# Polysketch attention and an ELU layer on one core: the first two query groups by squares of sums and differences

## The chip, the cores and the metric

One core of a Trainium2 chip. The metric is device time in microseconds (us) of one execution; lower is better. Work is shared by five engines with queues of their own: TensorE (PE, matrix products; PEld are its weight loads), VectorE (DVE), ScalarE (ACT), GpSimd (POOL) and SyncE (SP), which issues most transfers. SBUF is the working memory of 128 partitions; matmuls write to PSUM, which has eight banks of 128 x 512 fp32.

## The reference

Inputs: q, k, v of shape (4, 4, 1088, 32) in fp32, two sketches S1 and S2 of 8 x 32, and the two weights of the dense layer, 128 x 2048 and 2048 x 128. The sketches and the dense weights arrive as 64-bit floats (the divisions by a NumPy square root make them so).

```python
def phi(x):
    a = np.einsum('rd,bhsd->bhsr', S1, x)
    b = np.einsum('rd,bhsd->bhsr', S2, x)
    return np.einsum('bhsi,bhsj->bhsij', a, b).reshape(*x.shape[:-1], r * r)
q_p, k_p = (phi(q), phi(k))
kv = np.einsum('bhsf,bhsd->bhfd', k_p, v)
z = np.sum(k_p, axis=2)
num = np.einsum('bhsf,bhfd->bhsd', q_p, kv)
den = np.einsum('bhsf,bhf->bhs', q_p, z)[..., None] + 1e-06
attn = num / den
x = attn.transpose(0, 2, 1, 3).reshape(B * S, H * D)        # 4352 x 128
h = x @ w_in
g = np.where(h > 0.0, h, np.exp(np.minimum(h, 0.0)) - 1.0)
return g @ w_out
```

So each token has 64 features per head, the products of 8 sketch values a_i with 8 sketch values b_j.

## The kernel before

**Tiling.** The 4352 tokens are 68 half tiles of 64, taken in groups of eight (512 tokens): g = 0 to 7 are two groups for each batch element, and a last group holds the four half tiles left over. The 2048 hidden units are eight steps cp of 256, so a step (g, cp) is `mm1` (L840: two 128-unit halves into two PSUM banks, each in four 32-column tiles by `quarters`, L253), `elu_a` (L854: relu and exp on ScalarE), `elu_d` (L865: one VectorE instruction that writes gg) and `mm2` (L876) or a scheme with seven products (L770). The weights come as 64-bit words and are rounded on the chip: RA (VectorE, L102), RB (ScalarE, L107), RS, RM, RD, RE (VectorE, L117, L121, L129, L137). Number i of RA(i) and the others counts pieces: 0 and 1 are the first weight (w_in) of steps 0 and 1, 2 and 3 their second (w_out), 4 and 5 the two of step 2, and from 6 on whole steps.

**Order.** The order on each engine is written out by hand (`manual_schedule`): the order of the calls in the program is the order of every engine's queue. From L946 to L1000 stands the prologue: keys of batch element 0 are turned (`transp`, L279) and sketched (`KF`, L336), their products are formed (`KO_pool` on GpSimd, `KO_first` on VectorE, L416), z is summed (`Z_first`, `Z`, `Z_out`, which writes the third part of SW, L465), and kv is summed in the bank tagged o1 (`KA`, L428).

**Groups 0 and 1.** `q1_first` and `q1z_first` (L505, L517) or `q1_second` (L526) sketch the queries with tokens on the 128 partitions. `q2_den` (L581) makes the denominator, its reciprocal and an, the sketch a divided by it. `q2_out` (L599) forms the 64 products per token and head on VectorE (qp). `q4_early` (L612) turns qp by eight transposes on TensorE, copied out by ScalarE (L622). `q5_early` (L624) multiplies by kv (`KS_first`, L479, turns kv), and ScalarE copies the result to xg (L634), the input of `mm1`. `keep_warm` (L260) issues filler matmuls. Then `mm1_first` (L847) is step (0, 0), followed in the prologue by (0, 1) and the first `mm2`.

**After the prologue** the loop at L1108 runs the remaining steps from (1, 0) on, with `mm2` two steps behind `mm1`; `KT_out` (L441) of batch element 0 turns kv out of PSUM on VectorE and writes it to DRAM for later groups. Groups from 2 on get their queries in another way (`queries`, L706), between steps.

PSUM banks are handed out by tag: h (four), aux (two), o0 and o1 (one each); a new tile of a tag waits for the readers of the one it replaces.

Of the kernel before, what the change touches and what calls it, by code (L numbers as in the profile page):

```python
# [27 lines left out]
def kernel(  # L28
# [21 lines left out]
    nc = tc.nc  # L50
# [282 lines left out]
    kv_ps, feats, wzs, kf_ps = {}, {}, {}, []  # L333


    def KF(b):  # L336
# [91 lines left out]
    def KA(b, halves=(0, 1)):  # L428
# [4 lines left out]
        for i in range(0 if 0 in halves else 5, KT if 1 in halves else 5):  # L433
# [51 lines left out]
    NH = B * NT
    NQ = (NH + 7) // 8
# [9 lines left out]
    def half_tile(g, k):  # L496
        return (g // 2, 8 * (g % 2) + k) if g < NQ - 1 else (k, NT - 1)


    def q1_first():  # L500
        p = psum.tile([P, 512], F32, name="abqp", tag="aux")
        for i in range(4):
            for u in range(2):
                b, t = half_tile(0, 2 * i + u)
                nc.tensor.matmul(p[64 * u:64 * u + 64, i * 64:i * 64 + 64], qT[b][:, t, :],  # L505
                                 Sab[:].rearrange("p h y -> p (h y)"),
                                 skip_group_check=True, tile_position=(0, 64 * u))
        abw[0] = work.tile([P, H * 4, 2 * R], F32, name="abq", tag="abq", bufs=1)
        nc.scalar.copy(abw[0][:].rearrange("p (h t) y -> p h t y", h=H),
                       p[:, :256].rearrange("p (t h y) -> p h t y", t=4, h=H))  # L510

    def q1z_first():
        p = psum.tile([P, 512], F32, name="zqp", tag="h", bufs=4)
        for i in range(4):
            for u in range(2):
                b, t = half_tile(0, 2 * i + u)
                nc.tensor.matmul(p[64 * u:64 * u + 64, i * 32:i * 32 + 32].rearrange("p (h r) -> p h r", h=H),  # L517
                                 qT[b][:, t, :], SW[:, :, 2, :], skip_group_check=True, tile_position=(0, 64 * u))
        return p[:, :128].rearrange("p (t h r) -> p h t r", t=4, h=H)

    def q1_second():
        p = psum.tile([P, 512], F32, name="abwp", tag="h", bufs=4)
        for i in range(4):
            for u in range(2):
                b, t = half_tile(1, 2 * i + u)
                nc.tensor.matmul(p[64 * u:64 * u + 64, i * 96:i * 96 + 96], qT[b][:, t, :],  # L526
                                 SW[:].rearrange("p h x r -> p (h x r)"), skip_group_check=True,
                                 tile_position=(0, 64 * u))
        abw[1] = work.tile([P, H * 4, 3 * R], F32, name="abw1", tag="abq1", bufs=1)
        nc.scalar.copy(abw[1][:].rearrange("p (h t) y -> p h t y", h=H),  # L530
                       p[:, :384].rearrange("p (t h y) -> p h t y", t=4, h=H))
# [67 lines left out]
    def q2_out(g, parts=1, between=None):  # L599
        m = H * qn[g]  # L600
        x, an = abw.pop(g), ans.pop(g)
        qp[g] = work.tile([P, 4 * H, R, R], F32, name="qp", tag="qp", bufs=2)
        for i in range(parts):
            if i and between:
                between()
            h = slice(i * m // parts, (i + 1) * m // parts)
            a_ = an[:, h]
            b_ = x[:, h, :R]
            nc.vector.tensor_mul(qp[g][:, h], _ap(a_, list(a_.ap[1:]) + [[0, R]]),  # L609
                                 _ap(b_, [b_.ap[1], [0, R], b_.ap[2]]))  # L610

    def q4_early(g):  # L612

        qpT[g] = work.tile([P, H, 2, P], F32, name="qpT", tag="qpT", bufs=2)
        for hh in range(2):
            p = psum.tile([P, 512], F32, name="qtp", tag="aux")
            for h2 in range(2):
                for m in range(2):
                    o = (h2 * 2 + m) * P
                    r = (2 * hh + h2) * 4 + 2 * m  # L620
                    nc.tensor.transpose(p[:, o:o + P], qp[g][:, r:r + 2].rearrange("p t i j -> p (t i j)"), ident[:])  # L621
            nc.scalar.copy(qpT[g][:, 2 * hh:2 * hh + 2], p[:].rearrange("p (h m s) -> p h m s", h=2, m=2))  # L622

    def q5_early(g):  # L624
        xp = [psum.tile([P, 512], F32, name="xps", tag="aux") for _ in range(2)]
        for h in range(H):
            for w in range(2):
                nc.tensor.matmul(xp[w][D * h:D * h + D, :256], kvS[64 * w:64 * w + 64, h, :],  # L628
                                 qpT[g][64 * w:64 * w + 64, h].rearrange("p m s -> p (m s)"),
                                 skip_group_check=True, tile_position=(64 * w, D * h))  # L630
        xg[g] = work.tile([P, 512], F32, name="xg", tag="xg", bufs=3)
        to = xg[g][:].rearrange("p (m w s) -> p w m s", w=2, s=P)
        for w in range(2):
            nc.scalar.copy(to[:, w], xp[w][:, :256].rearrange("p (m s) -> p m s", s=P))  # L634
# [211 lines left out]

    def mm1_first():  # L847
        hs[0, 0] = [psum.tile([P, 512], F32, name="h", tag="h", bufs=4) for c in range(2)]
        for w in range(2):
            for c in range(2):  # L850
                cols = [x[:].rearrange("p (m w s) -> p w m s", w=2, s=P)[:, w] for x in (hs[0, 0][c], xg[0])]
                quarters(cols[0], W[:, 0, c * P:c * P + P], cols[1])
# [351 lines left out]
```

## Time and profile before

| | |
|---|---|
| median of 3 runs | 261.91 us (261.74 to 262.23) |
| the profiled execution | 262.34 us |
| its span, first to last instruction | 260.6 us |
| granted TensorE clock | 0.998 |
| first `mm1` starts | 16.25 us |
| first `mm2` ends | 23.51 us |
| busy: PE, DVE, ACT, POOL | 254.8, 186.9, 183.4, 159.0 us |

How to read it: an instruction row has its start and duration in us, the engine, the line of the kernel, the operation, output<-input by the program's names, and the shape. "x16" counts instructions; an fp32 matmul call is two of them, a transpose one. "[0.45 <-ACT e L863]" is idle time ahead of the instruction and what ended it. A chain of waits is followed back from the last instruction: each step names what the next one waited for. A busy PE need not be one at its peak, as matmuls are pipelined and their ends are modelled.

### The profile page before, as it was taken

The page shows a single profiled execution, that of the slowest core. Times are in us where ns is not written, and L with a number is a line of the kernel's source. Part 1 is how long each engine was busy: PE and PEld are TensorE (multiplying, and loading weights), DVE is VectorE, ACT ScalarE, POOL GpSimd, SP SyncE. Part 2 cuts the span into 40 slices and gives each one's busy share as a digit, 9 for nine tenths or more (in the row PEclk, how much of TensorE's full clock was granted, in tenths as well). Part 3 has the DMA queues.
Part 4 walks back from the last instruction along what each step waited for, and adds up shares of the span by engine and source line. Part 5 has one row for each costly group of instructions (what it writes and reads, how often), then busy time and mean ns, then how long its engine had stood idle before and what let it go on. Part 6 is the DMA issues. An engine that isn't in the chain of part 4 may idle for free.

```text
span 260.6 us, 9756 instructions
## 1 busy us (share of the span) xinstructions
PE 254.8 (98%) x4123; PEld 158.4 (61%) x4123; DVE 186.9 (72%) x352; ACT 183.4 (70%) x358; POOL 159.0 (61%) x202
## 2 busy tenths in 40 slices
PE   8899999999999999999999999999999999999994
PEld 6753333453346667666666666665666666668993
DVE  6799999999988967997477675744466746544651
ACT  2379968766667577776687777775877777777792
POOL 3520007002179996788678798888688888887310
PEclk9999999999999999999999999999999999999999
DMA  5998079012112210002100204220001110110021
GB/s 173 330 358 222 3 223 268 24 21 85 28 18 28 31 34 18 3 15 34 20 0 4 33 10 104 60 30 13 3 3 27 34 26 3 25 19 3 3 30 33
DMA packets 30379, 15.61 MB, mean 60 GB/s; under 512 B 22496, under 2 KB 28000, under 8 KB 30336
## 3 DMA queue, kind: packets, MB, share of 16 engines
q1 hardware_dynamic: 29904, 14.63, 23.0%
q8 instruction: 32, 0.52, 0.9%
q10 hardware_dynamic: 368, 0.30, 0.3%
q0 software_dynamic: 64, 0.07, 0.1%
q14 instruction: 11, 0.09, 0.1%
HBM read 11.31 MB, written 2.36 MB: 52 GB/s over the span
## 4 chain that ended last, share of the span: by engine, by line
PE 97%; DVE 1%; ACT 0%; issue 0%; DVEq 0%
PE h L256 45%; PE pb L790 17%; PE pa L790 13%; PE o L256 5%; PE pb L766 4%; PE ol L256 3%; PE idle L264 1%; PE kv L435 1%; PE abp L343 1%; PE h L681 1%; PE h L551 1%; PE qtp L621 1%; DVE qp L609 1%; PE h L693 1%; PE xps L628 0%; PE kfps L365 0%
## 5 line engine op out<-in xcount | busy, mean ns | idle before, releaser
L256 PE MATMUL h<-xg,W 128*32 128x512 f32 (+3 forms) x904 | 130.8, 539 | 0.4 <-ACT xg L634 0.4
L869 DVE SCALAR_TENSOR_TENSOR gg<-e,h 128x512 f32<-128x512 f32 x128 | 85.9, 681 | 52.6 <-ACT e L863 47.8
L861 ACT ACTIVATE e<-h 128x512 f32<-128x512 f32 x128 | 75.5, 590 | 46.2 <-PE h L256 46.0
L863 ACT ACTIVATE e<-e 128x512 f32<-128x512 f32 x128 | 80.9, 632 | 3.8
L751 POOL TENSOR_TENSOR tt<-gg 128x512 f32<-128x512 f32 x50 | 64.3, 1286 | 28.9 <-DVE gg L869 25.2
L256 PEld LDWEIGHTS h<-xg,W 128*32 128x32 f32 (+1 forms) x904 | 43.0, 122 | 43.0 <-issue 34.4
L754 POOL TENSOR_TENSOR tt<-gg,tt 128x256 f32<-128x256 f32 x50 | 36.9, 739 | 3.9
L753 POOL TENSOR_TENSOR tt<-tt,gg 128x256 f32<-128x256 f32 x50 | 36.7, 734 | 3.9
L790 PEld LDWEIGHTS pa<-gg,W 128*64 128x64 f32 (+1 forms) x496 | 23.7, 126 | 22.4 <-issue 22.2
L790 PE MATMUL pa<-gg,W 128*64 128x128 f32 (+1 forms) x496 | 30.6, 274 | 0.0
L790 PE MATMUL pb<-tt,SS 128*64 128x128 f32 (+1 forms) x480 | 29.6, 273 | 0.0
L790 PEld LDWEIGHTS pb<-tt,SS 128*64 128x64 f32 (+1 forms) x480 | 22.8, 126 | 0.0
L790 PE MATMUL pa<-tt,SS 128*32 128x128 f32 (+1 forms) x288 | 21.2, 273 | 0.0
L790 PE MATMUL pb<-gg,SS 128*64 128x128 f32 (+1 forms) x256 | 19.9, 273 | 0.0
L790 PE MATMUL pb<-tt,W 128*64 128x128 f32 (+1 forms) x256 | 19.9, 273 | 0.0
L134 POOL TENSOR_TENSOR raw<-raw,tiny 128x512 f32<-128x512 f32 x1 | 1.0, 1041 | 24.7 <-DVE raw L129 24.7
L256 PE MATMUL o<-gg,W 128*32 128x512 f32 x128 | 15.3, 595 | 0.0
L790 PEld LDWEIGHTS pa<-tt,SS 128*32 128x32 f32 (+1 forms) x288 | 13.7, 124 | 0.0
L790 PEld LDWEIGHTS pb<-gg,SS 128*64 128x64 f32 (+1 forms) x256 | 12.8, 125 | 0.0
L790 PEld LDWEIGHTS pb<-tt,W 128*64 128x64 f32 (+1 forms) x256 | 12.8, 125 | 0.0
L766 PE MATMUL pb<-gg,W 128*32 128x256 f32 x192 | 11.5, 380 | 0.0
L921 DVE SCALAR_TENSOR_TENSOR gg<-e,h 128x256 f32<-128x256 f32 x16 | 6.6, 418 | 6.4 <-PE h L256 3.2
(163 smaller groups left out, 269.3 us busy)
## 6 DMA issues: line engine op xcount, KB each, us to landing
raw<-in_moe_w_in_dram SPq DMA_DIRECT2D x8, 256.0 KB, 6.3
raw<-in_moe_w_out_dram SPq DMA_DIRECT2D x8, 256.0 KB, 6.5
out_dram<-ob SPq DMA_DIRECT2D x112, 16.0 KB, 1.5
hd_k<-in_k_dram SPq DMA_DIRECT2D x3, 544.0 KB, 7.5
hd_q<-in_q_dram SPq DMA_DIRECT2D x3, 544.0 KB, 8.5
v<-in_v_dram SPq DMA_DIRECT2D x4, 288.0 KB, 7.1
v<-in_v_dram SPq DMA_DIRECT2D x4, 256.0 KB, 8.4
raw<-qpF SPq DMA_DIRECT2D x16, 64.0 KB, 2.0
```

Source lines behind the costliest of these rows:

```text
L256: nc.tensor.matmul(dst[c:c + tile], lhs[:, c:c + tile], rhs, skip_group_check=True, tile_position=(0, c), **kw)
L264: nc.tensor.matmul(idle[c:c + tile, :cols], ones[:, :tile], ones[:, :cols], skip_group_check=True, tile_position=(0, c))
L343: nc.tensor.matmul(ps[i // 5][64 * u:64 * u + 64, 64 * (i % 5):64 * (i % 5) + 64], kT[b][:, u * KT + i, :], Sab[:].rearrange("p h y -> p ( ...
L751: nc.gpsimd.tensor_tensor(_ap(t[:, 0], [[4 * P, 2], [P, 2], [1, P]]), _ap(gs[g, cp][:, 0, P:], [[4 * P, 2]] + us), _ap(gs[g, cp][:, 0], [[ ...
L753: nc.gpsimd.tensor_tensor(t[:, 1], t[:, 2], b11, op=ADD)
L754: nc.gpsimd.tensor_tensor(t[:, 3], b21, t[:, 1], op=SUB)
L766: nc.tensor.matmul(acc[1][0][r:r + width[0], 256 * hi:256 * hi + 256], lhs[:, w:w + width[0]], gg[:, c, 256 * u:256 * u + 256], start=(cp ...
L790: nc.tensor.matmul(bank[r:r + width[0], P * col:P * col + P], lhs[:, w:w + width[0]], rhs[:, u], start=(first and i in ((0,) if g == 1 els ...
L861: nc.scalar.activation(e, hs[g, cp][c][:, :n], RELU, scale=-1.0)
L863: nc.scalar.activation(e, e, EXP, scale=-1.0)
L869: nc.vector.scalar_tensor_tensor(gs[g, cp][:, c, :n], es[g, cp][:, c, :n], -1.0, hs[g, cp][c][:, :n], op0=ADD, op1=MAX)
L921: nc.vector.scalar_tensor_tensor(gs["last", k // 2][:, k % 2, :2 * P], es["last", k // 2][:, k % 2, :2 * P], -1.0, hs["last", k][:, :2 * P ...
```

## The change

It uses 4ab = (a+b)^2 - (a-b)^2. For groups 0 and 1 the feature products are no longer formed on VectorE. `make_Spm` builds, on VectorE, weights whose 128 columns are the 64 sums S2_i + S1_j and the 64 differences, on all four heads' 32 rows. `q_sums` multiplies them with the queries as they lie (32 dimensions of a head on 32 partitions): four matmuls of 32 rows by 128 columns, a head each, side by side in the array. `q_squares` squares each result from PSUM to SBUF on ScalarE. kv stands twice on the 128 partitions, scaled by +1/4 and -1/4 (`KS_copy`), so `x_sums` needs one matmul of 128 rows per head. The denominator still comes from sketches with tokens on the partitions (`az`, `den_a`, `den_b`); `den_out` brings its reciprocal to the layout of x by 16 small matmuls with the identity, `den_copy` takes it to SBUF, and `x_out` on VectorE multiplies it in while it writes xg. The transposes, the fillers from `Z_out` on, and the copies to xg go. `KA` is cut in two, the squares and weight roundings are woven in between in a new order, `KT_out(0)` reads the SBUF copy of kv, and the second half of the q transpose comes earlier.

```diff
+    quarters_pm = const.tile([P, 1], F32, name="qpm")
+    nc.gpsimd.memset(quarters_pm[:64], 0.25)
+    nc.gpsimd.memset(quarters_pm[64:], -0.25)
...
+    def make_Spm():
+        for s, op in enumerate((ADD, SUB)):
+            nc.vector.tensor_tensor(Spm[:, s], _ap(sps[:, R:], [[1, R], [0, R]]), _ap(Sc[:], [[0, R], [1, R]]), op=op)
...
-        nc.vector.transpose(kt[:], kv_ps[b][:, :R * R])
+        nc.vector.transpose(kt[:], kv_ps[b][:, :R * R] if b else kds[0][:, 0])
...
+    def KS_copy():
+        nc.scalar.mul(kvS[:].rearrange("p h d -> p (h d)"), kv_ps[0][:, 128:256], quarters_pm[:])
...
+    def q_sums(g, half=None):
+        c = slice(0, 512) if half is None else slice(256 * half, 256 * half + 256)
+        for h in range(H):
+            if not half:
+                tag = "o0" if h == 3 else "h" if g or h == 2 else "aux"
+                sums[g, h] = psum.tile([P, 512], F32, name="qs", tag=tag, bufs={"o0": 1, "h": 4, "aux": 2}[tag])
+            rows = slice(32 * h, 32 * h + 32)
+            nc.tensor.matmul(sums[g, h][:, c], Spm[rows].rearrange("p s i j -> p (s i j)"),
+                             tokens(g, rows, c.start // 64, c.stop // 64), skip_group_check=True, tile_position=(32 * h, 0))
+
+    def q_squares(g, h):
+        if h % 2 == 0:
+            sq[g, h // 2] = work.tile([P, 2, 512], F32, name="sq", tag=("qp", "qpT")[g], bufs=2)
+        nc.scalar.square(sq[g, h // 2][:, h % 2], sums.pop((g, h))[:])
...
+    def az_copy(g):
+        abw[g] = work.tile([P, H, 4, R], F32, name="aq", tag=f"aq{g}", bufs=1)
+        nc.scalar.copy(abw[g][:], dens[g][:, :, :, 0, :])
...
+    def den_out(g, **kw):
+        ps = rbs[g] = psum.tile([P, 512], F32, name="rb", **kw)
+        for t in range(4):
+            for h in range(H):
+                nc.tensor.matmul(ps[32 * h:32 * h + 32, P * t:P * t + P], _ap(dens[g][:, 4 * h + t:], [[0, D]]), ident[:],
+                                 skip_group_check=True, tile_position=(0, 32 * h))
...
+    def x_sums(g, parts, half, **kw):
+        if half == 0:
+            xp[g] = psum.tile([P, 512], F32, name="xps", **kw)
+        c = slice(512 // parts * half, 512 // parts * (half + 1))
+        for h in range(H):
+            nc.tensor.matmul(xp[g][D * h:D * h + D, c], kvS[:, h, :], sq[g, h // 2][:, h % 2, c],
+                             skip_group_check=True, tile_position=(0, D * h))
+
+    def x_out(g, parts, half):
...
+        nc.vector.tensor_mul(xg[g][:, c], xp[g][:, c], rb_all[0][:, g, c])
...
     transp(qT, "q", 0, 0, 8)
-    zps, zl = Z_first()
-    q1_first()
+    make_Spm()
+    q_sums(0, 0)
+    zps = Z_first()
+    zl = ZC(0, zps)
     KO_pool()
     KO_first(4, 5)
     KO_first(5, 7)
+    q_sums(0, 1)
     Z(0, zps, zl)
+    q_squares(0, 0)
+    KA_first((4, 5, 6), True)
     Z_out(0, zps)
     KO_first(7, KT)
-    keep_warm(1, 96, 64)
-    zq = q1z_first()
-    q2_den(0, zq, lambda: RA(0))
-    q2_out(0, 2, lambda: RA(1))
-    KA(0)
-    KS_first()
-    keep_warm(1)
+    q_squares(0, 1)
+    az(0, zps)
+    KA_first((0, 1, 2, 3, 7, 8), False)
+    RA(0)
+    az_copy(0)
+    q_squares(0, 2)
+    transp(qT, "q", 0, 8, NT)
     RB(0)
+    den_a(0)
+    den_b(0)
+    az(1)
+    KS_kd()
+    q_squares(0, 3)
+    KS_turn()
+    den_out(0, tag="aux", bufs=2)
+    az_copy(1)
+    RA(1)
+    RS(0)
+    den_a(1)
+    den_b(1)
+    for f in (RM, RD, RE):
+        f(0)
+    KS_copy()
+    den_copy(0)
+    q_sums(1)
+    x_sums(0, 2, 0, tag="aux", bufs=2)
+    x_sums(0, 2, 1)
+    den_out(1, tag="o1", bufs=1)
     RB(1)
-    q4_early(0)
-    transp(qT, "q", 0, 8, NT)
-    RC_2()
-    RE(0)
-    RE(1)
-    q1_second()
-    q5_early(0)
-    keep_warm(1, 192, width[0])
+    for h in range(H):
+        q_squares(1, h)
+    x_out(0, 2, 0)
+    x_out(0, 2, 1)
     mm1_first()
-    q2(1, 2, lambda: RA(2))
+    RA(2)
     RB(2)
-    elu_a(0, 0, 0)
-    elu_a(0, 0, 1, (0,))
-    mm1(0, 1, (0,))
-    q4_early(1)
+    for f in (RS, RM, RD, RE):
+        f(1)
+    RA(3)
+    for f in (RS, RM, RD, RE):
+        f(2)
+    elu_a(0, 0, 0, (0,))
+    den_copy(1)
+    elu_a(0, 0, 0, (1,))
+    elu_a(0, 0, 1)
+    x_sums(1, 1, 0, tag="aux", bufs=2)
+    mm1(0, 1)
     elu_d(0, 0, 0)
-    mm1(0, 1, (1,))
-    elu_a(0, 0, 1, (1,))
-    RC(2)
-    RA(3)
-    elu_a(0, 1, 0, (0,))
+    x_out(1, 1, 0)
     RB(3)
-    q5_early(1)
     elu_d(0, 0, 1)
     mm2(0, 0, True, False)
```

More of the change, by code (lines that the diff above doesn't have):

```diff
@@ L304 @@
     nc.gpsimd.tensor_copy(SW[:, :, :2, :].rearrange("p h x r -> p h (x r)"), Sab[:])
+    Sc = const.tile([FD, R], F32, name="Sc")
+    nc.scalar.copy(Sc[:], sps[:, :R])
+    Spm = const.tile([FD, 2, R, R], F32, name="Spm")
+    def make_Spm():
+        for s, op in enumerate((ADD, SUB)):
+            nc.vector.tensor_tensor(Spm[:, s], _ap(sps[:, R:], [[1, R], [0, R]]), _ap(Sc[:], [[0, R], [1, R]]), op=op)
     Sxp = const.tile([FD, 2, 2, R], F32, name="Sxp")
@@ L332 @@
     kvd = {b: dram.tile([P, 2 * D], F32, name=f"kvd{b}")[:] for b in range(B)}
-    kv_ps, feats, wzs, kf_ps = {}, {}, {}, []
+    kv_ps, feats, wzs, kds, kf_ps = {}, {}, {}, {}, []
     def KF(b):
@@ L439, in KA, with KA_first @@
                 z_tile(b, kv, i)
+    def KA_first(tiles, first):
+        if first:
+            kv_ps[0] = psum.tile([P, 512], F32, name="kv", tag="o1", bufs=1)
+        for i in tiles:
+            for h in range(H):
+                nc.tensor.matmul(kv_ps[0][32 * h:32 * h + 32, :R * R], vt[0][:, (h * KT + i) * D:(h * KT + i + 1) * D],
+                                 feats[0, i // 5][:, i % 5, h].rearrange("p i j -> p (i j)"),
+                                 start=(first and i == tiles[0]), stop=(not first and i == tiles[-1]),
+                                 skip_group_check=True, tile_position=(0, 32 * h))
     def KT_out(b):
         kt = work.tile([P, 2 * D], F32, name="kvt", tag="kvt")
-        nc.vector.transpose(kt[:], kv_ps[b][:, :R * R])
+        nc.vector.transpose(kt[:], kv_ps[b][:, :R * R] if b else kds[0][:, 0])
         nc.sync.dma_start(kvd[b], kt[:])
@@ L476, in Z_first, with KS_kd, KS_turn @@
             z_tile(0, ps, i)
-        return ps, ZC(0, ps)
-    def KS_first():
-        kd = work.tile([P, 2, R * R], F32, name="kd", tag="kd", bufs=1)
+        return ps
+    def KS_kd():
+        kd = kds[0] = work.tile([P, 2, R * R], F32, name="kd", tag="kd", bufs=1)
         nc.scalar.copy(kd[:], _ap(kv_ps[0][:, :R * R], [[0, 2], [1, R * R]]))
-        nc.tensor.transpose(kv_ps[0][:, 128:256], kd[:].rearrange("p w f -> p (w f)"), ident[:])
-        nc.scalar.copy(kvS[:].rearrange("p h d -> p (h d)"), kv_ps[0][:, 128:256])
+    def KS_turn():
+        nc.tensor.transpose(kv_ps[0][:, 128:256], kds[0][:].rearrange("p w f -> p (w f)"), ident[:])
+    def KS_copy():
+        nc.scalar.mul(kvS[:].rearrange("p h d -> p (h d)"), kv_ps[0][:, 128:256], quarters_pm[:])
     NH = B * NT
@@ L497, in half_tile, with tokens @@
         return (g // 2, 8 * (g % 2) + k) if g < NQ - 1 else (k, NT - 1)
-    def q1_first():
-        p = psum.tile([P, 512], F32, name="abqp", tag="aux")
+    sums, sq, dens, rbs, xp = {}, {}, {}, {}, {}
+    rb_all = {}
+    def tokens(g, rows, t0=0, t1=8):
+        b, t = half_tile(g, t0)
+        return qT[b][rows, t:t + t1 - t0, :].rearrange("p t s -> p (t s)")
+    def q_sums(g, half=None):
[7 more added lines that the diff above has]
+                             tokens(g, rows, c.start // 64, c.stop // 64), skip_group_check=True, tile_position=(32 * h, 0))
@@ L502, in q1_first, with az @@
+    def q_squares(g, h):
+        if h % 2 == 0:
+            sq[g, h // 2] = work.tile([P, 2, 512], F32, name="sq", tag=("qp", "qpT")[g], bufs=2)
+        nc.scalar.square(sq[g, h // 2][:, h % 2], sums.pop((g, h))[:])
+    def az(g, p=None):
+        if p is None:
+            p = psum.tile([P, 512], F32, name="azp", tag="h", bufs=4)
         for i in range(4):
             for u in range(2):
-                b, t = half_tile(0, 2 * i + u)
-                nc.tensor.matmul(p[64 * u:64 * u + 64, i * 64:i * 64 + 64], qT[b][:, t, :],
-                                 Sab[:].rearrange("p h y -> p (h y)"),
+                b, t = half_tile(g, 2 * i + u)
+                nc.tensor.matmul(p[64 * u:64 * u + 64, 128 + i * 64:192 + i * 64].rearrange("p (h y) -> p h y", h=H),
+                                 qT[b][:, t, :], SW[:, :, 1:, :].rearrange("p h x r -> p h (x r)"),
@@ L507, in q1_first @@
                                  skip_group_check=True, tile_position=(0, 64 * u))
[L508 to L531, printed above, removed]
+        dens[g] = p[:, 128:384].rearrange("p (t h x r) -> p h t x r", t=4, h=H, x=2)
@@ new lines, in az_copy, with den_a, den_b @@
+    def az_copy(g):
+        abw[g] = work.tile([P, H, 4, R], F32, name="aq", tag=f"aq{g}", bufs=1)
+        nc.scalar.copy(abw[g][:], dens[g][:, :, :, 0, :])
+    def den_a(g):
+        pw = pws[g % 2]
+        nc.vector.tensor_mul(pw[:, :4 * H, :R].rearrange("p (h t) r -> p h t r", h=H), abw.pop(g)[:], dens[g][:, :, :, 1, :])
+    def den_b(g):
+        pw = pws[g % 2]
+        den = dens[g] = work.tile([P, 4 * H], F32, name="dn", tag="den", bufs=2)
+        nc.vector.tensor_reduce(den[:], pw[:, :4 * H], axis=AX, op=ADD)
+        nc.vector.reciprocal(den[:], den[:])
@@ new lines, in den_out, with den_copy @@
+    def den_out(g, **kw):
[3 more added lines that the diff above has]
+                nc.tensor.matmul(ps[32 * h:32 * h + 32, P * t:P * t + P], _ap(dens[g][:, 4 * h + t:], [[0, D]]), ident[:],
+                                 skip_group_check=True, tile_position=(0, 32 * h))
+    def den_copy(g):
+        if not rb_all:
+            rb_all[0] = work.tile([P, 2, 512], F32, name="rbc", tag="kp", bufs=3)
+        nc.scalar.copy(rb_all[0][:, g], rbs.pop(g)[:])
@@ new lines, in x_sums @@
+    def x_sums(g, parts, half, **kw):
[6 more added lines that the diff above has]
+    def x_out(g, parts, half):
+        if half == 0:
+            xg[g] = work.tile([P, 512], F32, name="xg", tag="xg", bufs=3)
+        c = slice(512 // parts * half, 512 // parts * (half + 1))
+        nc.vector.tensor_mul(xg[g][:, c], xp[g][:, c], rb_all[0][:, g, c])
@@ L575, in q1_out @@
                                 ps[r][:, o:o + 32 * m])
-    def q2(g, parts=1, between=None):
-        q2_den(g, None, between)
-        q2_out(g, parts)
     def q2_den(g, zq=None, between=None):
@@ L597, in q2_den @@
         ans[g] = an
[L599 to L634, printed above, removed]
     exch = [raw_2[:, c].bitcast(F32).rearrange("p (e m a) w -> p e m (a w)", e=2, a=16) if wide else
@@ L848, in mm1_first @@
         hs[0, 0] = [psum.tile([P, 512], F32, name="h", tag="h", bufs=4) for c in range(2)]
[L849 to L852, printed above, removed]
+        for c in range(2):
+            for w in range(2):
+                quarters(hs[0, 0][c][:, 256 * w:256 * w + 256], W[:, 0, c * P:c * P + P], xg[0][:, 256 * w:256 * w + 256])
     def elu_a(g, cp, c, parts=(0, 1)):
@@ L954 @@
     KO_first(5, 7)
+    q_sums(0, 1)
     Z(0, zps, zl)
+    q_squares(0, 0)
+    KA_first((4, 5, 6), True)
     Z_out(0, zps)
     KO_first(7, KT)
-    keep_warm(1, 96, 64)
-    zq = q1z_first()
-    q2_den(0, zq, lambda: RA(0))
-    q2_out(0, 2, lambda: RA(1))
-    KA(0)
-    KS_first()
-    keep_warm(1)
-    RB(0)
-    RB(1)
-    q4_early(0)
-    transp(qT, "q", 0, 8, NT)
-    RC_2()
-    RE(0)
-    RE(1)
-    q1_second()
-    q5_early(0)
-    keep_warm(1, 192, width[0])
+    q_squares(0, 1)
[5 more added lines that the diff above has]
+    transp(qT, "q", 0, 8, NT)
+    RB(0)
+    den_a(0)
[18 more added lines that the diff above has]
+    den_out(1, tag="o1", bufs=1)
+    RB(1)
+    for h in range(H):
+        q_squares(1, h)
+    x_out(0, 2, 0)
+    x_out(0, 2, 1)
     mm1_first()
-    q2(1, 2, lambda: RA(2))
+    RA(2)
     RB(2)
-    elu_a(0, 0, 0)
-    elu_a(0, 0, 1, (0,))
-    mm1(0, 1, (0,))
-    q4_early(1)
-    elu_d(0, 0, 0)
-    mm1(0, 1, (1,))
-    elu_a(0, 0, 1, (1,))
-    RC(2)
-    RA(3)
-    elu_a(0, 1, 0, (0,))
+    for f in (RS, RM, RD, RE):
[9 more added lines that the diff above has]
+    mm1(0, 1)
+    elu_d(0, 0, 0)
+    x_out(1, 1, 0)
     RB(3)
-    q5_early(1)
     elu_d(0, 0, 1)
     mm2(0, 0, True, False)
-    RA(4)
     for f in (RS, RM, RD):
         f(3)
-    elu_a(0, 1, 0, (1,))
+    RA(4)
+    elu_a(0, 1, 0)
     elu_a(0, 1, 1)
```

## The prediction

> **What bounds the kernel now.** I read the page's chain shares first, then the chain in order of time up to 60 us, then the busy time by stretch, then each engine's timeline up to 34 us. The page's chain:
>
> ```profile
> PE 97%; DVE 1%; ACT 0%; issue 0%; DVEq 0%
> ```
>
> TensorE carries the end almost alone. The chain in order of time (start, us, what) shows from where:
>
> ```profile
> 12.50 0.70 DVE qp L609
> 13.20 0.14 issue
> 13.34 0.63 PE qtp L621 x4
> 13.96 0.85 PE abwp L526 x16
> 14.81 0.70 PE xps L628 x16
> 15.52 0.64 ACT xg L634 x2
> 16.15 0.10 issue
> 16.25 2.79 PE h L256 x40
> 19.04 1.02 PE qtp L621 x8
> 20.07 0.99 PE h L256 x8
> 21.06 0.59 PE xps L628 x16
> 21.65 1.85 PE o L256 x16
> 23.51 3.43 PE h L256 x32
> ```
>
> Up to 16.25 us the chain changes engines; from there every link is TensorE. The first `mm2` (o) ends at 23.51, and after it come only steps that the change leaves alone. So the question is when that `mm2` ends, and whether VectorE and ScalarE keep up afterwards. Busy time by stretch (length, then PE, PEld, DVE, ACT, POOL, clock, DMA):
>
> ```profile
> 16.25:23.51 7.26, 7.26 (x92) 3.27 (x96) 6.88 (x20) 6.07 (x13) 0.00 (x0) 1.00 1.06 315
> 23.51:60.00 36.49, 36.49 (x515) 14.71 (x507) 35.10 (x63) 28.82 (x53) 5.36 (x5) 1.00 0.42 118
> ```
>
> TensorE never idles there, but VectorE has only 0.4 us to spare in the first stretch: it will decide as soon as TensorE gets faster. The VectorE timeline of one rounded weight half and the first wait later on:
>
> ```profile
> 19.70 0.42 DVE L117 SCALAR_TENSOR_TENSOR W<-raw,W 128x256 uint32<-128x256 uint32 x1
> 20.16 0.30 DVE L121 TENSOR_SCALAR raw<-raw 128x256 uint32<-128x256 uint32 x1
> 20.50 0.44 DVE L129 SCALAR_TENSOR_TENSOR raw<-raw 128x256 f32<-128x256 uint32 x1
> 20.97 0.43 DVE L137 SCALAR_TENSOR_TENSOR W<-raw,W 128x256 f32<-128x256 f32 x1
> 29.39 0.69 DVE L869 SCALAR_TENSOR_TENSOR gg<-e,h 128x512 f32<-128x512 f32 x1 [0.45 <-ACT e L863]
> ```
>
> The first four, start to start, are one half: 0.44+0.33+0.46+0.35 = 1.6 us. VectorE catches up only at 29.39.
>
> **Unknown: the new matmuls.** `q_sums` issues four 32-row by 128-column matmuls of 512 columns. No such tile is in the trace; the nearest, 16 tiles of 32x32 into four banks, on TensorE's timeline:
>
> ```profile
> 60.00 0.40 PE L551 MATMUL h<-qT,SWs 32*32 32x256 f32 x2
> 60.33 0.39 PE L551 MATMUL qps<-qT,SWs 32*32 32x256 f32 x2
> 60.65 1.93 PE L256 MATMUL o<-gg,W 128*32 128x512 f32 x16
> ```
>
> All 16 are over in 0.65 us. Eight 512-column calls of L256 take 1.72 in four tiles side by side, so 256 columns stream in 0.43; the other 0.22 is the change of tile shape (kfps L365, 288 columns: 0.65 against 0.48, so 0.17). Four 32x128 tiles fill the same array and the same four banks. Bounds for 512 columns: 0.86 side by side, 4 x 0.86 = 3.44 in turn. I take 0.86 plus 0.2, as all 16 tiles ran at once, and 0.6 for each half of group 0.
>
> The Trainium skill, TensorEngine Tiling (Array Packing), Key Properties, says that any change of tiling mode drains the array. The row here shows 128-row tiles going from 64 to 32 columns with no gap (zqp L517 from 9.57 for 0.66, kv L435 starting at 10.15). By the rule the two extra changes of that kind (the first `KA` is cut in two by `az`) cost some 0.4 us more and the gain below would be about 1.0 instead of 1.4; by the row nothing.
>
> **Other new prices**, from nearest rows. Square 128x512: 0.59 (copy L622 0.588, relu L861 0.583, exp L863 0.634). `az`, 16 instructions of 64 columns: 0.65 (L505 0.61 on the chain, L517 0.68). `den_out`, 32 instructions of 128 columns in four tiles: 0.86 (L790, 0.22 per 8); its stationary operand is one column repeated, which no row shows; a load takes 0.10 to 0.18 (L628, L343) and hides under the streaming; below that there is nothing to gain. `x_sums`: 0.86 whole, 0.43 a half. `x_out`: 0.69 whole, 0.42 a half (L869, L921), some 0.08 less back to back. `make_Spm`: two of 0.23 (L303). `az_copy`, `KS_copy`: 0.27 (L483); its scale pointer at most 0.13 more (L107 0.505 against L509 0.37). `den_a`, `den_b`: 0.3+0.33+0.29 as now.
>
> **Part by part.** On TensorE the change removes q1_first 0.61, q1z 0.68, four stretches of transposes (0.66+0.63+1.02), q1_second 0.85, two q5 (0.70+0.59) and filler, and adds, for each group, sums, `az`, `den_out`, `x_sums`. VectorE loses `an` and `qp` of both groups (2 x 1.7) and gains Spm 0.4, `x_out` 0.8 and 0.6, and 0.5 for rounding two weight halves apart instead of at once (L117, L121, L129 at 512 columns): 1.1 less. ScalarE loses 4.3 (abq 0.37, four L622 2.35, abw 0.48, four xg 1.3 less overlap) and gains 8 x 0.57 + two den copies 1.2 + 0.7: about 2.2 more.
>
> Free: `make_Spm` falls into VectorE's idle 7.06 to 7.80 (it waits for abk), without which it would cost 0.45. The two new POOL memsets (0.1 each, 0.03 apart) delay ident by under 0.1, and VectorE then waits for raw_s until 2.49 anyway; uncovered they would cost that 0.1. No DMA moves, nor any order on the SP queue; issues there that wait for a buffer follow VectorE, which is earlier. Arrivals: v at 3.3+5.6 = 8.9, needed 9.4; the second half of q lands by 10.28 (an SP issue of that time waited for it), needed 10.5; w_in of step 1 by 10.96, needed 12.1. The q transpose now stands ahead of `den_a(0)` on VectorE: were q late, `den_a(0)`, `den_out`, all of TensorE behind it would be too. `KT_out(0)` reads SBUF, so bank o1 comes free before mm2_blocks: the first pb took 1.85 instead of 1.73, 0.1 gained.
>
> **The new timeline**, hand-offs 0.1 (xg to h: 16.15 to 16.25).
> - TensorE: abp ends 7.78; sums half 8.35; zps 0.3, 8.65; sums half 9.25; Z 9.4; `KA` 24 x 16.8 ns (1.21/72) 9.8; `az(0)` 10.5; `KA` rest 0.81, 11.3; `az(1)` 11.95; turn of kv, waiting for its copy, 12.45; `den_out(0)` 13.35; `q_sums(1)` 14.4; `x_sums(0)` with a shape change 15.35; `den_out(1)` 16.2; first mm1 17.9; `x_sums(1)` 18.8; mm1(0,1) 20.5; first half of mm2 21.35.
> - ScalarE: squares 9.3 to 10.45; az copy 10.85; square 11.4; RB(0) 11.8; kv copy 12.07; square 12.6; az copy 12.85; den copy 13.95; RB(1) 14.4; four squares 16.7; RB(2) 17.2; relu, den copy, exp, relu, exp to 20.1.
> - VectorE: SW 9.7 (now 9.51, as two sums stand before it), kp 10.3, RA, transpose 11.25, den 12.1, RA(1), RS(0) 12.75, `den_a(1)` behind the az copy 12.95, den 13.87, rest of half 0 15.0, `x_out` 15.8, RA 16.0, half 1 17.6, RA, half 2 19.4, gg 20.0, `x_out(1)` 20.6, second gg 21.25.
>
> So the second half of mm2 starts at 21.35 and ends at 22.2, against 23.51: 1.3 earlier, where TensorE and VectorE arrive together. Behind it VectorE has the same work and is 0.95 ahead of now (21.25 for 22.2), TensorE 1.3. It needs no wait: mm1(1,1)'s second tile, wanted at 24.7, needs gg of (0,1) by VectorE at 24.2; ScalarE leads by 1.5, and VectorE's 0.45 idle at 29.39 goes. With 0.1 from pb: **1.4 us gained**. The new order waits for SW at `az(0)`, behind which all of TensorE stands; that is in the times above.
>
> The profiled execution took 262.34 us (span 260.6 and 1.74 around it), which becomes 260.9; the median of the runs shown is 0.43 below it, 261.91, so I forecast **260.5 us**, own range 260.0 to 261.0 (starts 0.4 earlier or later on both engines).
>
> **Rivals.**
> - *VectorE gives part back.* Its wait for the az copy, behind a fuller ScalarE, or q landing 0.3 later, pushes its 8.3 us line from 12.95 on one for one. For: 6.88 of 7.26 busy. Against: 0.2 slack at q. Gain 0.2 to 0.9: 261.0 to 261.7. 18%.
> - *Everything tighter.* No shape-change cost (three sums, 0.55) and den 0.4 earlier: gain 1.8 to 2.2, 259.7 to 260.1. Against: 0.17 and 0.22 in two rows. 6%.
> - *The tall tiles take turns* (the slower side). Place: `q_sums`, ahead of Z and of the first mm1. Price 2 x 2.58 = 5.2, less 1.4: 265.7. It decides from 1.4 us over the 2.25 counted, when the three calls take 3.65. For: no 128-column row tile in the trace. Against: 16 small tiles side by side. 8%.
> - *Square needs another activation table.* The only load (L155) took 1.28; it would come before the first square and the first exp. The first moves VectorE's line by 1.25, the second delays the second gg by 0.4 more: 22.9, mm2 ends 23.85, so about 262.1. Against: relu, copy and exp share one load in the whole trace. 4%. The Trainium skill, ScalarE: Activation LUTs, Table sets, says that cheap functions are in every set, without naming square among them; it would remove this case.
> - *The clock falls* as fillers go: every stretch shows 1.00, the least busy (1.61 of 2.00 us, 10 to 12) too; the longest new gap is 0.25. Half a clock for 3 us: 262.0 or more. 2%.
>
> **Numbers.** Forecast 62%. 0.2% is 0.5 us, about what a measurement here can tell. Faster: 62 + 6 + half of the first rival, 77%; same: its other half and half of the table case, 11%; slower 12%. The range 259.7 to 261.8 holds the forecast and the first two rivals, 86%, and leaves out the last three.
>
> **What would show it.** The three sums in 0.6, 0.6, 1.05 us; first mm1 at about 16.2 with TensorE unbroken from 12.45; mm2 ending at 22.2 with a wait under 0.1 for gg; no second table load; the chain TensorE's from there with links as now. Wrong if mm2 waits over 0.5 for VectorE, if a sum takes over 1.5, or if the lead at 23.5 melts by 60 us.

## The result and the profile after

| | before | after |
|---|---|---|
| median of 4 runs, taken side by side | 261.86 us (261.74 to 262.23) | 264.45 us (264.05 to 265.97) |
| the profiled execution, and its span | 262.34, 260.6 | 264.57, 262.8 |
| first `mm1` starts | 16.25 | 19.06 |
| first `mm2` ends | 23.51 | 25.80 |
| span after that | 237.1 | 237.0 |

The change costs 1.1%: ratio 1.0107, 95% interval 1.0066 to 1.0149. 260.5 us had been forecast. The last two rows place the loss: the first `mm2` ends 2.29 us later, and behind it nothing changes. The chain's shares by engine, on the page of after:

```profile
PE 94%; DVE 2%; issue 1%; ACT 1%
```

The chain in order of time, after (start, us, what):

```profile
12.38 0.26 PE kv L506
12.64 1.00 PE rb L579 x28
13.64 2.25 issue
15.89 0.41 PE rb L579 x4
16.30 1.11 PE qs L541 x8
17.41 1.07 ACT sq L547 x2
18.48 0.03 issue
18.51 0.76 DVE xg L599 x2
...
22.81 0.68 DVE gg L893
23.49 0.60 DVE xg L599
24.09 0.60 DVE gg L893
24.70 0.04 issue
24.74 1.06 PE o L259 x8
25.80 3.43 PE h L259 x32
```

Two things were not in the forecast. The first is the row of 2.25 us: `den_out(0)` (rb) has issued 28 of its 32 matmul instructions, then TensorE does nothing, waits for nothing that the profile shows, and then issues the last four. The second: from 18.51 to 24.70 the chain is VectorE's, where it should have been TensorE's; the second half of `mm2` waits for gg. The longest waits of TensorE and VectorE up to 30 us, one row from each table (us in total, times, longest):

```profile
PE rb L579 <- issue: 2.3, 1, 2.3
```

```profile
DVE xg L599 <- ACT sq L547: 3.5, 1, 3.5
```

After's busy time by stretch (length, then PE, PEld, DVE, ACT, POOL, clock, DMA share, GB/s), from the first `mm1` to the end of `mm2` and as far behind it as was shown of before:

```profile
19.06:25.80 6.74, 6.61 (x84) 2.27 (x80) 6.47 (x18) 6.25 (x12) 0.00 (x0) 1.00 0.94 230
25.80:62.29 36.49, 36.49 (x531) 14.93 (x537) 35.27 (x65) 28.25 (x51) 5.33 (x5) 1.00 0.38 109
```

VectorE has 0.27 us to spare in the first stretch: what it is late with at 18.51 it can't make up before `mm2`.

**What the 2.25 us are.** The page lists transfers that the program does not issue, marked "instruction": on queue q8 there are 32 of them with 0.52 MB, so 16 KB each, in both kernels. One of them starts just before the stop. The queue's row (packets, MB, share of the 16 engines), after from 13 to 14 us and before from 12 to 13:

```profile
q8 instruction: 1, 0.02, 6.8%
```

```profile
q8 instruction: 1, 0.02, 7.2%
```

In the trace it runs from 13.48 to 14.57 in after and from 12.81 to 13.97 in before. TensorE's records (matmuls and weight loads, one each) up to the stop, and in before up to the filler at 15.34 us (the same columns, PE and PEld with their counts first):

```profile
0.00:13.66 13.66, 12.24 (x219) 9.32 (x220) 9.75 (x37) 6.12 (x16) 6.60 (x30) 1.00 0.86 256
```

```profile
0.00:15.33 15.33, 13.61 (x221) 10.41 (x221) 11.60 (x37) 6.03 (x14) 7.16 (x28) 1.00 0.87 268
```

After stops when 439 matmuls and loads have gone. Before has issued 442 by 15.33, 1.36 us after its packet's end, and goes on. **Theory F:** TensorE's instructions arrive in packets of 16 KB; the program's early part needs a new one after some 440 records; the packet comes late because the loads of the weights fill the DMA (share 0.86 up to the stop), and TensorE goes on only 1.3 us after its end (14.57 to 15.89). Before reaches that count 1.7 us later, since its fillers, transposes and waits take time but few records, and escapes by a hair. **Rival D:** the stop belongs to `den_out`, whose stationary operand, a column repeated, is in no other row.

### The profile page after: what moved, and what is told of

The parts are those of the page before. It is cut to its first block, busy times and chain, and to the rows that moved or that the text cites. A ratio compares the mean times of both kernels' runs of the same rounds, so it can differ in the third digit from the quotient of the medians.

```text
span 262.8 us, 9832 instructions
## 1 busy us (share of the span) xinstructions
PE 255.3 (97%) x4157; PEld 158.1 (60%) x4157; DVE 185.7 (71%) x354; ACT 184.8 (70%) x361; POOL 157.9 (60%) x204
## 4 chain that ended last, share of the span: by engine, by line
PE 94%; DVE 2%; issue 1%; ACT 1%
PE h L259 43%; PE pb L815 16%; PE pa L815 13%; PE o L259 5%; PE pb L791 4%; PE ol L259 3%; PE idle L267 1%; PE kv L447 1%; PE qs L541 1%; PE h L706 1%; PE abp L355 1%; PE h L618 1%; PE rb L579 1%; DVE xg L599 1%; PE h L718 0%
## 5 line engine op out<-in xcount | busy, mean ns | idle before, releaser
L815 PEld LDWEIGHTS pa<-gg,W 128*64 128x64 f32 (+1 forms) x496 | 23.7, 126 | 22.4 <-issue 22.2
```

The lines of the kernel that those rows point to most:

```text
L815: nc.tensor.matmul(bank[r:r + width[0], P * col:P * col + P], lhs[:, w:w + width[0]], rhs[:, u], start=(first and i in ((0,) if g == 1 els ...
```

## The experiments

Each kernel's median stands with its ratio to before, timed beside it (261.88 to 262.0 us). "Stop" is TensorE's idle time by "issue"; the last column is the span behind the first `mm2`, in the profiled executions. The expectations speak of the 449th record; counted as above, TensorE stops behind the 439th to 442nd.

| kernel | median (range), runs | ratio, 95% interval | stop | `mm2` ends | span behind |
|---|---|---|---|---|---|
| e1_hold | 262.04 (261.72 to 263.76), 10 | 1.0011 [0.9995, 1.0027] | 0.33 | 23.95 | 236.9 |
| e2_wide_den | 267.6 (267.0 to 268.2), 4 | 1.0213 [1.0189, 1.0237] | none | 29.48 | 236.9 |
| e3_before_more | 263.03 (262.76 to 263.29), 5 | 1.0037 [1.0024, 1.0051] | 1.14 | 24.41 | 237.1 |
| e4_few | 268.07 (267.8 to 268.79), 4 | 1.0228 [1.0211, 1.0245] | none | 29.53 | 237.5 |
| e5_hold_order | 261.83 (261.73 to 262.96), 10 | 1.0005 [0.9992, 1.0017] | none | 23.03 | 237.0 |
| e6_wide_copy | 262.53 (262.04 to 263.75), 10 | 1.0032 [1.0016, 1.0049] | none | 24.89 | 236.9 |
| e7_swap | 263.43 (263.17 to 263.59), 4 | 1.0054 [1.0039, 1.0069] | 1.10 | 24.85 | 236.9 |
| e8_before_hold | 262.32 (262.07 to 262.73), 10 | 1.0015 [1.0005, 1.0024] | none | 23.49 | 237.1 |
| e9_best | 262.22 (261.39 to 263.5), 12 | 1.0009 [0.9996, 1.0023] | none | 22.91 | 236.9 |
| e10_order_only | 265.51 (265.33 to 266.65), 4 | 1.0142 [1.0126, 1.0158] | 1.90 | 26.59 | 237.0 |
| e11_whole | 261.42 (261.06 to 262.42), 12 | 0.9982 [0.9972, 0.9992] | inside `q_sums(1)` | 23.58 | 236.9 |
| e12_after_again | 265.81 (264.4 to 266.23), 4 | 1.0134 [1.0109, 1.016] | 2.17 | 26.89 | 237.0 |

**e1: hold the loads back.** In after, all loads behind w_in of step 1 wait until GpSimd has made the key products (a one-element write to the buffer of the next load, behind them on GpSimd's queue). If the packet is late because of them, the stop shrinks; if `den_out` itself stops, it stays.

```diff
+    def load_rest():
+        nc.gpsimd.memset(raw_2[:, 1, 2 * P:2 * P + 1, :].bitcast(F32), 0.0)
+        load_w(1, 1)
+        load_w(0, 1)
...
     KO_pool()
+    load_rest()
     KO_first(4, 5)
```

> The changed kernel with one difference: every load behind the first weight of step 1 is held on the SP queue until GpSimd has finished its key products (near 9.8 us), by a one-element write to its target. Theory F (TensorE ran out of instructions; the transfer that brings the next ones stood behind data): the instruction packet of 16 KB that started at 13.48 us in the changed kernel starts at 11.5 us or earlier, the idle stretch in L579 shrinks from 2.25 us to under 0.7, and the time falls by 1.3 to 2.3 us, to 262.2 to 263.2. Rival D (something in den_out itself, its repeated-column weight loads or a wait for dn): the gap of 2.2 us stays in L579 and the time stays at 264.4 or rises by what the later loads cost.

The packet moved from 13.48 to 11.85, and the same four matmuls resume after 0.33. TensorE's timeline (start, us, then the shape and, in brackets, idle time ahead):

```profile
12.77 0.94 PE L581 MATMUL rb<-ident,dn 128*32 128x128 f32 x24
14.04 0.41 PE L581 MATMUL rb<-ident,dn 128*32 128x128 f32 x4 [0.33 <-issue]
```

So 1.92 of the 2.25 us were the packet's lateness, and the median falls by 2.4. What is left is a second loss, since 262.04 is still no faster than before. VectorE shows it, first e1 and then after:

```profile
16.66 0.76 DVE L601 TENSOR_TENSOR xg<-xps,rbc 128x256 f32<-128x256 f32 x2 [1.61 <-ACT sq L549]
```

```profile
18.51 0.76 DVE L599 TENSOR_TENSOR xg<-xps,rbc 128x256 f32<-128x256 f32 x2 [3.53 <-ACT sq L547]
```

Even with the stop nearly gone, VectorE stands idle for 1.61 us ahead of `x_out(0)`, with the rounding of the next two weight halves and two gg queued behind it. The rows name a square as the releaser, but it is only the event nearest in time. In all eight kernels with two halves in which VectorE waits here, `x_out` starts 0.11 to 0.14 us after the end of the *second* half of `x_sums(0)` (16.52 to 16.66 in e1), although its first half needs only the first; in e7, e11 and e12 that square ended at another time, and in e12 the row names `x_sums` (xps) itself. TensorE's row in e1, and VectorE's in e12:

```profile
15.45 1.07 PE L594 MATMUL xps<-sq,kvS 128*32 128x256 f32 x16
```

```profile
19.62 0.76 DVE L599 TENSOR_TENSOR xg<-xps,rbc 128x256 f32<-128x256 f32 x2 [4.91 <-PE xps L592]
```

**e2 and e4: another `den_out`, and fewer instructions.** e2 makes the reciprocal on 512 columns, so that `den_out` is four plain 128x128 calls, 8 matmul records for 32. e4 also halves the instructions of `az` and takes `x_sums(0)` whole.

```diff
-        nc.vector.reciprocal(den[:], den[:])
+        nc.vector.reciprocal(dens[g], _ap(den[:], [[1, 4], [4, H], [0, D]]))
...
-            for h in range(H):
-                nc.tensor.matmul(ps[32 * h:32 * h + 32, P * t:P * t + P], _ap(dens[g][:, 4 * h + t:], [[0, D]]), ident[:],
-                                 skip_group_check=True, tile_position=(0, 32 * h))
+            nc.tensor.matmul(ps[:, P * t:P * t + P], dens[g][:, t].rearrange("p h d -> p (h d)"), ident[:],
+                             skip_group_check=True)
```

> The changed kernel with den_out as four matmuls of 128x128 instead of sixteen of 128x32 for each group (VectorE writes the reciprocal repeated 32 times, some 0.4 us more there): 48 fewer TensorE records per group, the same streaming time. Theory F: TensorE again stops after about 449 of its records, now not in den_out but in x_sums of group 0 (L592 or near it), from about 15 us until 15.9 to 16.2: the gap shrinks to about 1 us and the time falls by about 1.0 us, to about 263.4. Rival D: den_out no longer stalls and nothing else does, so the time falls by the whole 2.2 us to 262.2; or, if it is the wait for dn, the gap of 2.2 stays in den_out.

> The changed kernel with den_out in four wide matmuls, az in four 128-column calls instead of eight of 64, and x_sums of group 0 whole: 48, 16 (for each group) and 16 records fewer. Theory F: the 449th record now falls into the first mm1, due at about 17 us, when the instructions are in: no idle stretch of TensorE over 0.5 us before mm2, the first mm1 starts at about 16.8 instead of 19.06, and the time falls by about 2.2 us to about 262.2, which would be level with the kernel before: the forecast gain of 1.4 us would then still be missing for another reason (x_out standing until both halves of x_sums are done, with VectorE idle and its weight rounding behind it). Rival D: as for the wide den_out alone, no difference between the two.

Both missed, and tell nothing of F or D: the reciprocal put a longer wait in the place of the stop. VectorE's timeline, e2 and then after:

```profile
13.39 3.35 DVE L575 RECIPROCAL dw<-dn 128x512 f32<-128x512 f32 x1
```

```profile
12.16 0.25 DVE L572 RECIPROCAL dn<-dn 128x16 f32<-128x16 f32 x1
```

3.35 us for 512 columns is 6.5 ns each; the wide gg of 512 columns takes 0.68. It runs twice ahead of the first `mm1`, and TensorE stood still for 3.02 us in e2 and 2.60 in e4. The granted clock fell to 0.50 as well, from 16.76 to 20.17 us in e2 and from 15.08 to 21.91 in e4, so their times hold that loss too (e12 comes back to it).

**e3: before, with more records.** The filler behind `KS_first`, one call of full width, becomes sixteen of 64 columns, four on each 32-column tile: 60 more records. F says that before then stops too; D says that it does not, as it has no `den_out`.

```diff
     KS_first()
-    keep_warm(1)
+    keep_warm(4, 64, 32)
     RB(0)
```

> The kernel before with the filler behind KS_first as 16 calls of 64 columns in 32-column tiles instead of one call of 256 columns: 60 more TensorE records for the same streaming time (0.43 us, perhaps 0.1 more). Theory F: the kernel before just escaped, its 449th record being due at 15.3 us when the packet that started at 12.81 us had been in for about a microsecond; with 60 more records it stops in q1_second (L526) from about 14.2 until about 15.3, and the time rises by 0.8 to 1.4 us, to 262.7 to 263.3. Rival D: only the filler's overhead, 0 to 0.2 us.

It stops, in a step that the change does not have, after 442 records. TensorE's timeline, and the stretch up to the resumption:

```profile
13.65 0.38 PE L526 MATMUL abwp<-SW,qT 128*64 128x96 f32 x2
15.17 0.87 PE L526 MATMUL abwp<-SW,qT 128*64 128x96 f32 x14 [1.14 <-issue]
```

```profile
0.00:15.16 15.16, 12.15 (x221) 9.29 (x221) 11.74 (x37) 5.62 (x13) 7.28 (x28) 1.00 0.87 266
```

Its packet began at 12.54, and 1.14 us of stop became 0.37% of the time. This settles F against D.

**e7: swap two steps.** `q_sums(1)`, eight matmuls and their loads (16 records) in 1.1 us, goes ahead of `den_out(0)`. F says that the stop stays at the count and so moves to an earlier matmul of `den_out`, and shrinks by what `q_sums` takes; D says that it stays behind the 28th.

```diff
     KS_turn()
+    q_sums(1)
     den_out(0, tag="aux", bufs=2)
...
     den_copy(0)
-    q_sums(1)
     x_sums(0, 2, 0, tag="aux", bufs=2)
```

> The changed kernel with one call moved: q_sums of group 1 stands ahead of den_out of group 0 on TensorE, so 1.05 us of long matmuls (16 records) come before the 449th record instead of behind it. Theory F: the stop stays at the same record, now the 12th or so of den_out's 32 matmuls, begins near 14.2 and ends where it ended, 15.9; the first mm1 starts 0.9 to 1.05 us earlier, and the time falls by 0.7 to 1.0 us, to 263.4 to 263.7. Rival D: den_out stops for 2.2 us wherever it stands, and the time stays at 264.4.

```profile
14.02 0.85 PE L579 MATMUL rb<-ident,dn 128*32 128x128 f32 x21
15.96 0.52 PE L579 MATMUL rb<-ident,dn 128*32 128x128 f32 x10 [1.10 <-issue]
```

On TensorE's timeline it is now ahead of the 22nd matmul of `den_out`, after 440 records, and 1.10 long: packet at 13.47 as in after, resumption at 15.96 as against 15.89. The instant of resumption stayed and the work ahead of it grew.

**e6: the wide reciprocal mended.** As e2, with a small reciprocal and a copy on VectorE that repeats it (0.43 us).

```diff
         nc.vector.reciprocal(den[:], den[:])
+        nc.vector.tensor_copy(dens[g], _ap(den[:], [[1, 4], [4, H], [0, D]]))
```

> The changed kernel with den_out as four matmuls of 128x128, the reciprocal taken on 16 columns as before and then repeated by a VectorE copy of 512 columns (some 0.45 us more on VectorE for each group). 48 TensorE records fewer in group 0's den_out. Theory F: TensorE's stop moves out of den_out into x_sums of group 0 (the 449th record), from about 15.3 to about 16; the time falls by 0.8 to 1.4 us, to 263.0 to 263.6. Rival D (the stop belongs to the narrow repeated-column loads): no stop anywhere, 262.6 or less.

No stop is left, and 1.9 us of after's loss are regained. By the expectations this is D's outcome: F had put a shorter stop into `x_sums`. It does not speak against F, though, for with 48 fewer records (24 matmuls and their loads) the count is reached at 16.9 us, 1.7 us after the packet's end at 15.14, and the other kernels went on 1.2 to 1.5 us after theirs. TensorE had also waited 1.8 us for Spm at the start of this execution, so that it alone does not tell F from D.

**e5, e9, e10: the second loss.** e5 is e1 with the next rounding (RS to RE of half 1) ahead of `x_out(0)`, in VectorE's idle time, and RB(1) on ScalarE ahead of the kv copy. e9 puts `den_a(1)` and `den_b(1)` behind the rounding of half 0, and only RS and RM of half 1 ahead of `x_out(0)`. e10 is e9 without e1's held loads. The edit that e9 and e10 share:

```diff
     RS(0)
+    for f in (RM, RD, RE):
+        f(0)
     den_a(1)
     den_b(1)
-    for f in (RM, RD, RE):
-        f(0)
+    RB(1)
     KS_copy()
...
-    RB(1)
     for h in range(H):
         q_squares(1, h)
+    RS(1)
+    RM(1)
     x_out(0, 2, 0)
     x_out(0, 2, 1)
+    RD(1)
+    RE(1)
     mm1_first()
...
-    for f in (RS, RM, RD, RE):
-        f(1)
```

> The kernel with held loads, and besides the rounding of the first weight of step 1 is put ahead of x_out of group 0 on VectorE (its ScalarE part ahead of KS_copy). With held loads VectorE stood idle for 1.61 us ahead of x_out, and the second gg (22.83) let mm2 wait. Theory G (the rest of the missing gain is VectorE's 6.2 us of work behind an x_out that waits for both halves of x_sums): the idle stretch is filled, the second gg ends near 21.8, mm2 ends near 23.3 instead of 23.95 with no wait over 0.1, and the time falls by 0.6 to 0.7 us, to 261.4. Rival P (TensorE's own work up to mm2 is the bound): mm2 ends no earlier than 23.8 and the time stays within 0.2 of 262.04.

> Held loads, the rounding of step 1's first weight begun ahead of x_out as in the run before, but only its first two instructions, and den_a and den_b of group 1 behind the rounding of step 0. In the run before, the first mm1 waited 0.37 us for x_out, which stood behind 1.6 us of rounding, and VectorE was busy without a break from 12.0 us on. Theory G: x_out starts at about 15.5 instead of 16.34, the first mm1 right behind den_out of group 1 at about 16.3 instead of 16.81, mm2 ends near 22.4 instead of 23.03, and the time falls by 0.5 to 0.7 us against that run, to 261.2, which is 0.7 below the kernel before. Rival P: TensorE finds another wait in its place (gg or the weights for mm2) and the time stays at 261.7 to 261.9.

> The same order as the run with this label's partner, but with the loads issued as in the changed kernel. Theory F: the stop of TensorE at its 449th record is back (2.0 to 2.3 us in den_out), the first mm1 starts near 18.2 to 19.0, and the time is 1.4 to 2.2 us above that of the partner, 262.8 to 263.5. If held loads helped in another way only, by the order of VectorE's work, the two would be within 0.5 us.

In e5 `mm2` no longer waits for gg, but it put too much ahead of `x_out`, and the first `mm1` waits 0.37 for it; its median is 0.2 below e1's and not 0.6. e9's chain (start, us, what) is the one that the forecast had in mind, TensorE's alone from 8.9 us to the end of `mm2`:

```profile
15.79 0.87 PE rb L581 x32
16.66 1.73 PE h L261 x32
18.39 0.86 PE xps L594 x8
19.25 1.72 PE h L261 x16
20.96 0.86 PE o L261 x8
21.82 0.02 issue
21.84 1.06 PE o L261 x8
22.91 3.43 PE h L261 x32
```

That execution took 261.62 us. Over twelve runs e9 lies between 261.39 and 263.5, its median not below e5's: the edit does what it should in the trace, but no gain over e5 is shown. e10 brings the stop back, 1.90 us after the same 439 records, as F says. It came out some 2 us slower than expected. In its profiled execution the start was late too (the full clock came at 9.98 us, against 4.13 in after), in a part that the edit does not touch. In its three other executions the mean clock was 0.994, as in the profiled one of e12 below; they have no trace.

**e8: the control.** Before, with the loads held as in e1.

> Control: the kernel before with the same loads held as in the changed kernel with held loads. Theory F: the kernel before hid its instruction transfer, so holding gains nothing: within 0.3 us of 261.9. If holding the loads were good by itself (by less contention for other transfers, say), it would fall by over 0.5 us.

It is 0.15% slower than before. In its trace `mm1` waits 0.66 us for a rounded weight half, and that rounding had stood 0.16 us until a held load landed; in before `mm1` waits 0.38, for xg. So holding is worth nothing by itself, and what e1 gains is the stop.

**e11: fewer records earlier.** e9 with `q_sums(0)` in one piece behind `Z_first`, four matmul calls for eight.

```diff
-    q_sums(0, 0)
     zps = Z_first()
+    q_sums(0)
...
-    q_sums(0, 1)
     Z(0, zps, zl)
```

> As the run with held loads and the finer order, but group 0's sums are taken in one piece of four 512-column matmuls behind Z_first, instead of two halves around it. The two halves took 0.83 and 0.64 us on the chain, the whole one of group 1 took 1.07, so TensorE, which the chain of that run names without a break from 7.8 us on, saves 0.4 us. Theory P (TensorE's work up to mm2 is now the bound): den_out starts near 12.3 instead of 12.64, mm2 ends 0.3 to 0.4 us earlier, the best runs fall to 261.0 to 261.1, and the median to 261.8. Rival S (what spreads these kernels' runs over 2 us is late arrival of q or a late TensorE clock, which this changes little): the fastest run improves by 0.3, and the spread stays. Rival G (VectorE still decides): no change.

It is the only kernel that beats both before and after: 0.9982 of before, interval 0.9972 to 0.9992, some 0.5 us, with nine of its twelve runs under 261.6. Its profiled execution, 262.31, is one of the two slowest; there `q_sums(1)` took 2.03 us where e9's took 1.07, at full clock, and the count falls into it: three of its four matmul calls began at 13.39, the fourth only at 14.36, 1.36 us behind the packet's end at 13.00. So this kernel still touches the stop.

**e12: after, once more.** The kernel unaltered, to see whether stop and count come back.

> The changed kernel again, unaltered. Theory F: TensorE stops once more behind 439 matmul and load records, for 1.7 to 2.4 us, and the time is 264.0 to 264.8. If the stop of the first profile was an accident of that execution, there is no gap over 0.5 us here, or one at another record.

They do: 2.17 us, after 439 records. But three of the four runs are above 265.6, and the profiled one of them (265.65) shows why. TensorE's timeline, and the busy time and clock of three stretches:

```profile
15.54 0.41 PE L579 MATMUL rb<-ident,dn 128*32 128x128 f32 x4 [2.17 <-issue]
15.88 1.74 PE L541 MATMUL qs<-qT,Spm 32*128 32x512 f32 x8
```

```profile
14.00:15.53 1.53, 0.00 (x0) 0.00 (x0) 0.68 (x2) 0.00 (x0) 0.00 (x0) 1.00 1.07 367
16.30:19.69 3.39, 3.39 (x33) 1.19 (x29) 0.07 (x1) 2.75 (x6) 0.00 (x0) 0.50 1.06 347
19.70:23.00 3.30, 3.30 (x73) 1.92 (x68) 3.16 (x10) 2.04 (x5) 0.00 (x0) 1.00 1.07 237
```

Behind the stop the granted clock is 0.50 from 16.29 to 19.70, so `q_sums(1)` takes 1.74 us instead of 1.14. In after's own profiled execution a stop of 2.25 us left the clock at 1.00. From the end of the stop to the end of `mm2` it is 11.35 us here and 9.91 in after, so a stop can cost 1.4 us on top of its length, by chance. The Trainium skill, TensorE: Matmul & The Clock Gate, What's actually happening, gives a free-running window of about 3.4 us that an idle TensorE must fill before its clock is halved. The 3.41 us at 0.50 agree with the window's length; the idle time does not, as 2.17 us were enough here. In the traces the clock changes only after whole multiples of 3.41 us (10.24 and 3.41 in e12). Counted from its changes, e12's stop falls into one such stretch, 12.88 to 16.29, and after's into two, with 0.73 us ahead of 14.37 and 1.52 behind it. That may be the difference; it was not tested, and in e4 the clock halved behind a stretch with 1.43 us of idle time.

## Why the prediction was wrong

- **The step that failed** is "first mm1 at about 16.2 with TensorE unbroken from 12.45", that is `den_out(0)` ending at 13.35. The sum for TensorE had only durations and waits for data. It had no term for the arrival of its own instructions, and removing fillers and waits brings the same records earlier: 439 of them by 13.64, where before takes until after 15. The stop of 2.25 us decides the sign of the result (e1, e3, e7, e10, e12). The trace of before held a hint: its packet ended at 13.97, and its margin by the resumption times of the others, 1.2 to 1.5 us behind the packet, was about zero.
- **The second step that failed** is on VectorE: "rest of half 0 15.0, `x_out` 15.8". In e1 half 0 is done at 15.05, but `x_out` starts at 16.66, and the second gg ends at 22.84 where 21.25 had been forecast: both are 1.6 us late. `x_out`'s first half waits for the whole of `x_sums(0)`, which the same text had end at 15.35; with the hand-off of 0.13 that makes 15.5, so the missed wait is 0.5 of the 1.6. The rest is that TensorE came later than forecast: the stop's 0.33, and the sizes below (in e9, without a stop, `x_sums(0)` ended at 15.79). The nearest of the rivals is "VectorE gives part back", but it had another wait, the one for the az copy, and its 261.0 to 261.7 does not reach e1's 262.04.
- **Sizes.** Of the three sums, forecast at 0.6, 0.6 and 1.05, the chain shows 0.85, 0.64 and 1.07 to 1.11. `den_out` was put at 0.86 and took 1.01 and 0.87, `x_sums(0)` 1.00 for 0.95. In e9 these put the first `mm1` at 16.66 on the chain instead of 16.2, and `mm2` at 22.91 instead of 22.2; 0.6 us of the 1.4 forecast are left.
- **Right:** the tall tiles run side by side (1.07 us, where turns would have taken 3.44). `az` took 0.68 for 0.65. The cut of `KA` by `az` cost 0.07 (on the chain 0.47 and 0.81 for 0.40 and 0.81), so the row was nearer than the 0.4 that had been estimated for the Trainium skill's rule (TensorEngine Tiling (Array Packing), Key Properties). Square cost no second table load (one of 1.28 us in the trace), and no POOL or SP step got in the way. Behind `mm2` nothing changed, 237.0 against 237.1 us, so nothing was lost or gained there.
- **The clock** was a rival at 2%, with a longest gap of 0.25 us. That gap was wrong by the stop; the halved clock itself appears in e2, e4 and e12.

With the loads held, the rounding moved into VectorE's wait and group 0's sums whole (e11), the change gains 0.5 us, a third of the 1.4 forecast.

## What to carry to other kernels

Count instructions as well as time at a program's start: while transfers fill the DMA, look for the instruction packets in the trace, and see how far the engine with the most instructions is from the end of the last packet. A filler or a wait that seems to be pure loss may be what keeps an engine behind its instructions. And a result made in two halves is worth it only if the reader's wait is for its half: look in the trace which end the reader follows.

## What the runs showed of the hardware

- TensorE can run out of instructions: it stopped after 439 (after, e10, e12), 440 (e7) and 442 records (e3), for 1.10 to 2.25 us. Resumption came 1.2 to 1.5 us after the end of the 16 KB packet, which itself took 1.0 to 1.2 us. The packet began 1.6 us earlier with the loads held (e1).
- What asks for the packet is not shown, but its start goes with TensorE's own progress. TensorE's 180th record came between 8.9 and 11.2 us; in the nine traces without held loads the packet followed it by 3.1 to 3.8 us, in the five with held loads by 0.6 to 2.4. Other records near the 180th fit as well.
- The clock can halve for 3.41 us after 2.17 us of idle time (e12), and need not after 2.25 (after).
- A VectorE reciprocal took 6.5 ns per column on 512 columns, five times the gg instruction on as many.
- Open: why the runs of the changed kernels spread over 1.4 to 2.1 us (e9, e11, e1), where before's spread 0.5 to 0.6. The time at which TensorE's clock comes up differed between executions (4.1 us in after, 6.9 in before, 10.0 in e10), but it was not tried whether that is the cause.
